# Grouped-query attention on one core: K by four heads, scores of two heads per matmul, by halves of the keys

## The chip, the core and the metric

The kernel runs on one core of a Trainium2 chip. TensorE (PE) multiplies; its weight loads have a queue of their own (PEld). VectorE (DVE), ScalarE (ACT) and GpSimd (POOL) do the rest, and SyncE (SP) issues every transfer between HBM and SBUF; 16 DMA engines carry them. The metric is the device time of one execution in microseconds, as the median of several runs. The kernel before takes 344.64 us (3 runs, 344.35 to 345.31).

## The reference

```python
B, Hq, Hkv, Sq, Sk, D = 16, 32, 8, 16, 2048, 128     # bfloat16
k = jnp.repeat(k, rep, axis=1)                        # rep = Hq // Hkv = 4
v = jnp.repeat(v, rep, axis=1)
scores = jnp.einsum("bhqd,bhkd->bhqk", q, k) * D ** -0.5
p = _softmax(scores, axis=-1)
return jnp.einsum("bhqk,bhkd->bhqd", p, v)
```

There are 16 x 8 = 128 K/V heads with 2048 keys each, 0.5 MB of K and 0.5 MB of V per head: 134 MB in all against 4 MB of Q and output. Each K/V head serves 4 query heads of 16 rows, so 64 query rows. Nothing is used twice, so all 134 MB go through SBUF once.

## The kernel before

Work goes by **pairs**: two K/V heads, 128 query rows, 64 pairs p in all. For a pair:

- SP loads K (`load_k`, L172; 1 MB, 8 KB in a row per partition) and V (`load_v`, L178; 1 MB, two rows of 4 KB per partition). The 64 partitions of one K head hold 32 keys each. V's last pair comes in two loads (`LASTV`). Q comes for eight pairs at once (`load_q`, 256 KB).
- DVE transposes K in blocks of 32 by 32 (`kt`, L315, two instructions of 1024 4-byte words per pair). A word is a pair of neighbouring bfloat16, so the two of a word, `e`, stay together, and `b` tells the two halves of 128 bytes apart. After it a 32-partition block of `KT` holds 32 words of D for its keys; the blocks 0 and 1 belong to the first head, 2 and 3 to the second, with different keys.
- GpSimd copies Q four times side by side into `Q4` (L165, once per eight pairs), so that PE's transposes (L246) put the same Q words in all four 32-partition blocks; ACT moves them to `QT` (L358).
- PE computes the scores S: for each of four accumulation steps (`b`, `e`) and two column halves `u`, four matmuls in tiles of 32 rows by 64 columns (L268 with a weight load, L224 on the loaded weights), one for each 32-partition block, into the whole of `S_ps` (4 of 8 PSUM banks).
- DVE scales by -1/sqrt(D), writes `Sneg` and accumulates the row minimum `nbias` (L333). ACT computes exp with that bias, writes `P` in bfloat16 and accumulates the row sum (L368). DVE inverts the sum (L324).
- PE transposes `P` in words (L280, eight per pair), ACT moves the result to `PT` (L378, two per pair). `PT` has `NPT` buffers, and PSUM has `NSTAGE` = 3 places for such transposes.
- PE multiplies `PT` with V (PV). In the wide form (L298) 16 matmuls of 256 columns compute each head's rows with both heads' V, and the useless halves are not read; ACT divides with two instructions (L391). In the narrow form (L304) 32 matmuls of 64 rows and 128 columns compute only what is needed; ACT divides with one (L395). The last `NFAST` = 12 pairs are narrow; the last pair is divided by DVE (L348).
- SP stores the 128 output rows (`store`, L198).

The order on PE and ACT is written out by a planner (L118 to L139) before the instructions are emitted. Iteration p puts S(p+1) first on PE, then PV(p-3) (`PVLAG`), then the transposes of P(p), and in four of eight iterations a part of the next Q. ACT gets exp(p), the division of p-3, the copies of P(p) and of Q. On DVE (L326 to L342) iteration p scales p, inverts p-1 and transposes K of p+2.

SP's order (L206 to L215) is fixed too: step t issues K of t, a Q if one is due, V of t-5 (`VLAG`), the store of t-12 (`SLAG`). SP waits in front of each until its buffer is free: K has 6 buffers (`NK`; free after both transposes), V has 8 (`NV`; free after PV), outputs 8. A wait there holds back all that is behind it. A load is one issue for all 16 DMA engines; its semaphore rises as each lands its share, so a load has landed when the last engine has.

Of the kernel before, what the change touches and what calls it, by code (L numbers as in the profile page):

```python
# [11 lines left out]
NK = 6  # L12
NV = 8
NKT = 2
NPT = 3
# [3 lines left out]
VLAG = 5  # L19
PVLAG = 3  # L20
SLAG = 12
QLEAD = 7
LASTV = ((0, 12), (12, 16))
NFAST = 12


def bass_standalone__gqa_softmax__sampling_kernel(
# [11 lines left out]
    NP = G // 2  # L39
    J = Sk // 128  # L40
# [9 lines left out]
    ident = sb("ident", [128, 128], BF16)  # L50
    ident4 = sb("ident4", [128, 128], F32)
    Kn = [sb(f"Kn{i}", [128, 2 * J * 128], BF16) for i in range(NK)]
# [5 lines left out]
    Sneg = [sb(f"Sneg{i}", [128, Sk], F32) for i in range(2)]  # L58
    P = [sb(f"P{i}", [128, Sk // 2], F32) for i in range(2)]
    PT = [sb(f"PT{i}", [128, J // 2, 128], F32) for i in range(NPT)]  # L60
    Osb = [sb(f"O{i}", [128, 128], BF16) for i in range(NO)]
    nbias = sb("nbias", [128, NP], F32)
# [15 lines left out]
    sem_max = sem("sem_max")  # L78
    sem_rec = sem("sem_rec")
# [10 lines left out]
    kf = k.rearrange("b h s d -> (b h s d)").rearrange("(n a x) -> n a x", n=NP, a=128)  # L90
    vf = v.rearrange("b h s d -> (b h) (s d)").rearrange("g (a x) -> a g x", a=128)

# [19 lines left out]
    def transposes(p):  # L112
        for h in range(2):
            u = stage("P", p, h)
            pe_prog.append(("PT", p, h, u))
            act_prog.append(("pe", p, h, u))
# [4 lines left out]
    for p in range(NP - 1):  # L121
        pe_prog.append(("S", p + 1))
        act_prog.append(("exp", p))
# [3 lines left out]
        transposes(p)  # L127
# [3 lines left out]
    for p in range(NP - 4, NP - 2):  # L131
        pv(p)
    act_prog.append(("exp", NP - 1))
    for p in range(NP - 4, NP - 2):
        norm(p)
    transposes(NP - 1)
# [15 lines left out]
    with nc.Block() as block:  # L152

        @block.gpsimd
        def _(gp):
            gp.iota(iota_t[:, :], [[1, 128]], base=0, channel_multiplier=-1).then_inc(sem_id, 1)
            gp.wait_ge(sem_id, 1)
            gp.tensor_scalar(ident[:, :], iota_t[:, :], 0.0, None, op0=ALU.is_equal).then_inc(sem_id, 1)
            gp.tensor_scalar(ident4[:, :], iota_t[:, :], 0.0, None, op0=ALU.is_equal).then_inc(sem_id, 1)
            for c in range(NQC):  # L160
                gp.wait_ge(sem_q[c % NQ], 16 * (c // NQ + 1))
                if c >= 1:
                    gp.wait_ge(sem_st, last_q[c - 1, 3] + 1)
                src = Qn[c % NQ][:, :, :].rearrange("p j (b x) -> p (j b) x", b=2)
                gp.tensor_copy(  # L165
                    Q4[:, :, :, :, :].rearrange("p j b r x -> p (j b) r x"),
                    src.unsqueeze(2).to_broadcast([128, 16, 4, 64]),
                ).then_inc(sem_q4, 1)

        @block.sync  # L170
        def _(sp):
            def load_k(p):  # L172
                s = p % NK
                if p >= NK:
                    sp.wait_ge(sem_kt, 2 * (p - NK) + 2)
                sp.dma_start(Kn[s][:, :], kf[p]).then_inc(sem_k[s], 16)
# [248 lines left out]
```

## Time and profile before

| | |
|---|---|
| median of 3 runs | 344.64 us (344.35 to 345.31) |
| the profiled execution | 344.92 us |
| its span in the profile | 343.1 us |
| instructions | 8217 |
| granted TensorE clock | 1.00 |
| mean rate of the loads | 405 GB/s |

The profile is of one execution. A row of the page names the line of the kernel, engine, operation, the tiles written and read, their partitions by elements and type, and the count; after the bar the total busy time and the mean duration in ns, then the time that the engine was idle just ahead of these instructions and what ended it. PE's matmuls are pipelined, so its busy time is an upper figure. A timeline line gives start, duration (merged, if it stands for several), engine, line and operation, and in brackets the idle time ahead of it with what ended it. The records of landings tell when each DMA engine had landed its share of a load. The chain that ended last, by engine:

```profile
PE 83%; DMA 5%; issue 4%; DVE 3%; ACT 1%; SPq 1%; POOL 1%; DVEq 0%; ACTq 0%
```

### The profile page before, as it was taken

The page shows a single profiled execution, that of the slowest core. Times are in us where ns is not written, and L with a number is a line of the kernel's source. Part 1 is how long each engine was busy: PE and PEld are TensorE (multiplying, and loading weights), DVE is VectorE, ACT ScalarE, POOL GpSimd, SP SyncE. Part 2 cuts the span into 40 slices and gives each one's busy share as a digit, 9 for nine tenths or more (in the row PEclk, how much of TensorE's full clock was granted, in tenths as well). Part 3 has the DMA queues.
Part 4 walks back from the last instruction along what each step waited for, and adds up shares of the span by engine and source line. Part 5 has one row for each costly group of instructions (what it writes and reads, how often), then busy time and mean ns, then how long its engine had stood idle before and what let it go on. Part 6 is the DMA issues. An engine that isn't in the chain of part 4 may idle for free.

```text
span 343.1 us, 8217 instructions
## 1 busy us (share of the span) xinstructions
PE 312.1 (91%) x3904; PEld 189.2 (55%) x2880; DVE 297.6 (87%) x321; ACT 291.8 (85%) x404; POOL 30.3 (9%) x15
## 2 busy tenths in 40 slices
PE   0757999999999999999999999999999999887784
PEld 0413656655665575557555755665565575454354
DVE  2289989999999999999899989998999898989840
ACT  1258899999999999999999999999988899877864
POOL 4500012000400004000300004000040000000000
PEclk9999999999999999999999999999999999999999
DMA  7999999999999999999999999999999999999993
GB/s 294 429 414 415 415 411 413 414 416 417 412 418 419 413 415 417 412 420 415 412 421 414 414 416 416 415 418 417 415 412 419 419 412 420 417 413 418 410 393 126
DMA packets 37300, 138.94 MB, mean 405 GB/s; under 512 B 11408, under 2 KB 11664, under 8 KB 29072
## 3 DMA queue, kind: packets, MB, share of 16 engines
q1 hardware_dynamic: 37264, 138.42, 99.6%
q8 instruction: 27, 0.44, 0.5%
q14 instruction: 9, 0.07, 0.1%
HBM read 136.31 MB, written 2.10 MB: 403 GB/s over the span
## 4 chain that ended last, share of the span: by engine, by line
PE 83%; DMA 5%; issue 4%; DVE 3%; ACT 1%; SPq 1%; POOL 1%; DVEq 0%; ACTq 0%
PE O_ps L298 28%; PE S_ps L268 18%; PE S_ps L224 15%; PE ST_ps L280 15%; PE ST_ps L246 5%; DMA Vb<-in_v_dram 4%; DVE KT L317 2%; PE O_ps L304 2%; DMA Qn<-in_q_dram 1%; DVE Sneg L333 1%; POOL Q L165 1%; SPq L204 1%; ACT P L368 1%; SPq L184 0%; PE S_ps L304 0%
## 5 line engine op out<-in xcount | busy, mean ns | idle before, releaser
L333 DVE TENSOR_SCALAR_CACHE_REDUCE Sneg<-S_ps 128x2048 f32<-128x2048 f32 x64 | 146.2, 2285 | 25.2 <-PE S_ps L224 24.0
L368 ACT ACTIVATE P<-Sneg,nbias 128x2048 bf16<-128x2048 f32 x64 | 158.8, 2481 | 7.7 <-DVE Sneg L333 6.1
L317 DVE STREAM_TRANSPOSE KT<-Kn 128x1024 f32<-128x1024 f32 x128 | 150.9, 1218 | 10.9 <-DMA Kn<-in_k_dram 10.9
L268 PE MATMUL S_ps<-KT,QT 32*64 32x512 bf16 x1024 | 103.4, 391 | 5.5 <-DVE Sneg L333 4.7
L224 PE MATMUL S_ps<-KT,QT 32*64 32x512 bf16 x1024 | 102.0, 385 | 0.0
L298 PEld LDWEIGHTS O_ps<-Vb,PT 128*128 128x128 bf16 x832 | 77.3, 98 | 44.0 <-issue 35.7
L298 PE MATMUL O_ps<-Vb,PT 128*128 128x256 bf16 x832 | 99.9, 273 | 1.5 <-issue 1.5
L378 ACT ACTIVATE PT<-ST_ps 128x512 f32<-128x512 f32 x128 | 69.5, 595 | 6.0 <-PE ST_ps L280 4.8
L280 PE MATMUL ST_ps<-ident,P 128*128 128x128 f32 x512 | 69.0, 278 | 2.8 <-ACT P L368 2.8
L268 PEld LDWEIGHTS S_ps<-KT,QT 32*64 32x64 bf16 x1024 | 30.0, 104 | 70.4 <-issue 61.6
L280 PEld LDWEIGHTS ST_ps<-ident,P 128*128 128x128 f32 x512 | 55.1, 141 | 12.1 <-ACT P L368 9.6
L391 ACT ACTIVATE O<-O_ps,rrec 64x128 bf16<-64x128 f32 x104 | 37.7, 363 | 15.8 <-PE O_ps L298 14.7
L165 POOL COPY Q<-Qn 128x4096 bf16<-128x4096 bf16 x8 | 28.8, 3602 | 224.2 <-PE ST_ps L246 143.9
L246 PE MATMUL ST_ps<-ident,Q 128*128 128x128 f32 x128 | 20.4, 291 | 10.1 <-POOL Q L165 10.1
L358 ACT ACTIVATE QT<-ST_ps 128x512 f32<-128x512 f32 x32 | 19.3, 603 | 10.0 <-PE ST_ps L246 10.0
L246 PEld LDWEIGHTS ST_ps<-ident,Q 128*128 128x128 f32 x128 | 16.4, 150 | 10.1 <-issue 10.1
L304 PE MATMUL O_ps<-Vb,PT 128*64 128x128 bf16 x288 | 9.8, 220 | 7.2 <-issue 7.2
L304 PEld LDWEIGHTS O_ps<-Vb,PT 128*64 128x64 bf16 x288 | 8.5, 110 | 12.9 <-issue 12.9
L324 DVE RECIPROCAL rrec<-rowsum 128x1 f32<-128x1 f32 x64 | 10.1, 158 | 3.1 <-ACT P L368 3.1
L368 ACT ACTIVATION_READ_ACCUMULATOR P<-Sneg,nbias 128x1 f32 x64 | 12.2, 190 | 0.0
L395 ACT ACTIVATE O<-O_ps,rrec 128x128 bf16<-128x128 f32 x9 | 3.3, 365 | 6.6 <-PE O_ps L304 6.6
L333 DVE DVE_READ_ACCUMULATOR Sneg<-S_ps 128x1 f32 x64 | 5.3, 83 | 0.0
(12 smaller groups left out, 10.2 us busy)
## 6 DMA issues: line engine op xcount, KB each, us to landing
Kn<-in_k_dram SPq DMA_DIRECT2D x64, 1024.0 KB, 15.9
Vb<-in_v_dram SPq DMA_DIRECT2D x63, 1024.0 KB, 17.7
Qn<-in_q_dram SPq DMA_DIRECT2D x8, 256.0 KB, 15.6
out_dram<-O SPq DMA_DIRECT2D x64, 32.0 KB, 15.9
Vb<-in_v_dram SPq DMA_DIRECT2D x1, 768.0 KB, 13.0
Vb<-in_v_dram SPq DMA_DIRECT2D x1, 256.0 KB, 12.5
```

The costliest lines, as they stand in the source:

```text
L165: gp.tensor_copy(Q4[:, :, :, :, :].rearrange("p j b r x -> p (j b) r x"), src.unsqueeze(2).to_broadcast([128, 16, 4, 64]),).then_inc(sem_q ...
L224: return pe.add_instruction(mybir.InstMatmult(name=nc.get_next_instruction_name(), engine=mybir.EngineType.PE, ins=[pe.lower_ap(rhs), pe.l ...
L246: ins = pe.transpose(dst[:, 128 * j:128 * (j + 1)], src[:, 4 * x + j, b, :], ident4[:, :])
L268: ins = pe.matmul(s_ap, w, x, start=(acc == 0), stop=(acc == 3))
L280: ins = pe.transpose(dst[:, 128 * t:128 * (t + 1)], P[p % 2][:, 128 * x:128 * (x + 1)], ident4[:, :])
L298: ins = pe.matmul(O_ps[:, 0:256], pt[:, j // 2, j % 2, :], Vb[p % NV][:, :, j, :], start=(j == 0), stop=(j == J - 1),)
L304: ins = pe.matmul(o_ap(p)[64 * g:64 * (g + 1), :], pt[:, j // 2, j % 2, 64 * g:64 * (g + 1)], Vb[p % NV][:, g, j, :], start=(j == 0), stop ...
L317: dve.transpose(KT[p % NKT][:, :].rearrange("p (t b e a x) -> p x e t b a", t=J // 2, b=2, e=2, x=2)[:, x, :, :, :, :], Kn[p % NK][:, :].b ...
L333: dve.tensor_scalar(Sneg[p % 2][:, :].rearrange("p (t h x) -> p h t x", t=8, h=2), S_ps[:, :].rearrange("p (h t x) -> p h t x", t=8, h=2), ...
L368: act.activation(P[p % 2][:, :].bitcast(BF16).rearrange("p (n y e) -> p n y e", n=16, e=2), Sneg[p % 2][:, :].rearrange("p (n e y) -> p n ...
L378: act.activation(PT[p % NPT][:, 4 * h:4 * (h + 1), :].rearrange("p t q -> p (t q)"), stage_ap(u), ACT.Copy,).then_inc(sem_ev, 1)
L391: ins = act.activation(Osb[p % NO][rows, :], O_ps[rows, 128 * g:128 * (g + 1)], ACT.Copy, scale=rrec[rows, p:p + 1])
```

## The change

K is loaded for **four heads** at a time: 2 MB, 16 KB in a row per partition, 32 loads in 3 buffers. A 32-partition block now belongs to one head and holds 64 keys per partition. So a block's words of D and keys are transposed as before, but the two blocks of 64 neighbouring partitions belong to two different heads, a pair. S is computed for two pairs (a **quad**, Q) by **halves of the keys**: step n = 2Q + x is half x of the keys of pairs 2Q and 2Q+1. One matmul takes 64 rows, the blocks of both heads of a pair, and 128 columns of weights. That the product of one head's queries with the other head's keys does not enter is seen to in Q's layout: each of `Q4`'s four copies is multiplied by a mask, 1 on the Q rows of its head and 0 on the others, so `QT` has zeros where query and key head differ. There are 64 steps S as before, each 16 matmuls of 512 columns (8 weight loads) in two tiles of 64 x 128, where there were 32 (16 weight loads) in four tiles of 32 x 64.

DVE now scales half a pair at a time (two instructions of 1024 per step instead of one of 2048), and after the second half takes the minimum of the two halves' minima for both pairs of the quad with one instruction, behind a wait for its own results. Only that releases exp of both pairs (`sem_nb`). The sums are inverted for two pairs at once. `Sneg` has 3 buffers instead of 2. exp reads its input in eight steps of 128 bytes, 32 times over, where it read two steps of 256 bytes, 64 times over; with that `P` has the keys in V's order.

The planner issues S two steps ahead instead of one, PV 4 behind instead of 3, V 6 behind instead of 5, stores 14 instead of 12; `PT` has 5 buffers instead of 3, V 7 instead of 8. Narrow are the last 8 pairs and before them each fourth. Q goes ahead of K in SP's first step. The last iterations are written out anew.

```diff
-NK = 6
-NV = 8
+NK = 3
+NV = 7
-NPT = 3
+NS = 3
+NPT = 5
-VLAG = 5
-PVLAG = 3
-SLAG = 12
+VLAG = 6
+PVLAG = 4
+SLAG = 14
-NFAST = 12
+NFAST = 8
+def both_heads(p, NP):
+    return p < NP - NFAST and p % 4 != 3
...
+    pe_prog.append(("S", 1))
+    for p in range(NP - 2):
+        pe_prog.append(("S", p + 2))
+        exp(p)
...
+    for p in range(NP - 2 - PVLAG, NP - 3):
         pv(p)
-    act_prog.append(("exp", NP - 1))
-    for p in range(NP - 4, NP - 2):
-        norm(p)
-    transposes(NP - 1)
+        if p < NP - 4:
+            norm(p)
+    exp(NP - 2)
+    exp(NP - 1)
+    ev = turn(NP - 2)
+    act_prog += ev
+    norm(NP - 4)
+    pv(NP - 3)
+    norm(NP - 3)
+    ev = turn(NP - 1)
+    act_prog += ev
     pv(NP - 2)
     norm(NP - 2)
     pv(NP - 1)
...
-                gp.tensor_copy(
-                    Q4[:, :, :, :, :].rearrange("p j b r x -> p (j b) r x"),
-                    src.unsqueeze(2).to_broadcast([128, 16, 4, 64]),
-                ).then_inc(sem_q4, 1)
+                for r in range(4):
+                    gp.tensor_scalar(
+                        Q4[:, :, :, r, :].rearrange("p j b x -> p (j b) x"), src,
+                        mask[:, r:r + 1], None, op0=ALU.mult,
+                    ).then_inc(sem_q4, 1)
...
+            def load_k(n):
+                s = n % NK
+                if n >= NK:
+                    sp.wait_ge(sem_kt, 4 * (n - NK) + 4)
+                sp.dma_start(Kn[s][:, :], kf[n]).then_inc(sem_k[s], 16)
...
+                            for y in range(2):
+                                rows = slice(64 * y, 64 * (y + 1))
+                                s_ap = S_ps[:, 512 * (2 * y + u):512 * (2 * y + u + 1)]
+                                w = qt[rows, b, e, 128 * (i + y):128 * (i + y + 1)]
+                                x = kt[rows, b, e, 2 * u:2 * (u + 1), :]
                                 if u == 0:
                                     ins = pe.matmul(s_ap, w, x, start=(acc == 0), stop=(acc == 3))
                                 else:
-                                    ins = matmul_on_loaded(s_ap, w, x, (32 * r, 64 * g), acc == 0, acc == 3)
+                                    ins = matmul_on_loaded(s_ap, w, x, (64 * y, 0), acc == 0, acc == 3)
...
+            for n in range(NP):
+                Q, x = divmod(n, 2)
+                dve.wait_ge(sem_s, n + 1)
+                for y in range(2):
+                    p = 2 * Q + y
+                    if x == 0 and p >= NS:
+                        dve.wait_ge(sem_exp, p - NS + 1)
+                    dve.tensor_scalar(
+                        Sneg[p % NS][:, 1024 * x:1024 * (x + 1)],
+                        S_ps[:, 1024 * y:1024 * (y + 1)], -scale, None,
+                        op0=ALU.mult, op1=ALU.min, accum_out=nhalf[:, x, p:p + 1],
+                    ).then_inc(sem_max, 1)
+                if x == 1:
+                    dve.wait_ge(sem_max, 2 * n + 2)
+                    pair = slice(2 * Q, 2 * Q + 2)
+                    dve.tensor_tensor(nbias[:, pair], nhalf[:, 0, pair], nhalf[:, 1, pair], op=ALU.min).then_inc(sem_nb, 1)
+                elif n >= 4:
+                    recip(Q - 2)
+                if n + 2 < NP:
+                    for e in range(2):
+                        kt(n + 2, e)
...
-                    act.wait_ge(sem_max, p + 1)
+                    act.wait_ge(sem_nb, p // 2 + 1)
...
-                        P[p % 2][:, :].bitcast(BF16).rearrange("p (n y e) -> p n y e", n=16, e=2),
-                        Sneg[p % 2][:, :].rearrange("p (n e y) -> p n y e", n=16, e=2), ACT.Exp,
+                        P[p % 2][:, :].bitcast(BF16).rearrange("p (n a m) -> p n a m", n=8, m=8),
+                        Sneg[p % NS][:, :].rearrange("p (n m a) -> p n a m", n=8, m=8), ACT.Exp,
```

The order of the instructions after the change, at the end, is on PE: S(63), PV(57), transposes of P(61), PV(58) to PV(60), transposes of 62, PV(61), transposes of 63, PV(62), PV(63); on ACT: exp(61), division 57, two copies of 61, divisions 58 and 59, exp(62), exp(63), two copies of 62, divisions 60 and 61, two copies of 63, division 62. In SP's order the last K load is followed by V of pairs 56 to 63.

## The prediction

> **What bounds the kernel now.** I read the page's busy shares first, then its DMA queues, then the busy time by stretches, then the timeline of the last 35 us.
>
> ```profile
> PE 312.1 (91%) x3904; PEld 189.2 (55%) x2880; DVE 297.6 (87%) x321; ACT 291.8 (85%) x404; POOL 30.3 (9%) x15
> q1 hardware_dynamic: 37264, 138.42, 99.6%
> q8 instruction: 27, 0.44, 0.5%
> L333 DVE TENSOR_SCALAR_CACHE_REDUCE Sneg<-S_ps 128x2048 f32<-128x2048 f32 x64 | 146.2, 2285 | 25.2 <-PE S_ps L224 24.0
> L368 ACT ACTIVATE P<-Sneg,nbias 128x2048 bf16<-128x2048 f32 x64 | 158.8, 2481 | 7.7 <-DVE Sneg L333 6.1
> L317 DVE STREAM_TRANSPOSE KT<-Kn 128x1024 f32<-128x1024 f32 x128 | 150.9, 1218 | 10.9 <-DMA Kn<-in_k_dram 10.9
> L165 POOL COPY Q<-Qn 128x4096 bf16<-128x4096 bf16 x8 | 28.8, 3602 | 224.2 <-PE ST_ps L246 143.9
> ```
>
> Four engines are at 85% or more and the loads are at 99.6%, so shares alone don't name the bound. The stretches do (time, then busy time of PE, PEld, DVE, ACT, POOL, then clock, DMA share, GB/s):
>
> ```profile
> 95.90:135.40 39.50, 39.50 (x465) 24.05 (x337) 37.17 (x41) 37.04 (x53) 3.60 (x1) 1.00 1.02 415
> 254.10:293.90 39.80, 38.59 (x452) 24.18 (x332) 36.18 (x40) 35.74 (x52) 1.06 (x1) 1.00 1.02 415
> 293.90:343.00 49.10, 36.91 (x696) 22.88 (x572) 34.01 (x39) 35.63 (x47) 0.00 (x0) 1.00 0.91 362
> ```
>
> Up to about 235 us PE is never idle: eight iterations take 39.5 us, 4.94 each. The loads run at 415 GB/s throughout. A pair is 2.10 MB of K and V plus 0.07 MB of Q and output, so loading it takes 5.2 us: PE is the faster of the two. It starts late, catches up, and from about 290 us DVE waits for K at each pair. So **the loads set the end**; PE sets it only in so far as it must have caught up. The end itself:
>
> ```profile
> 323.14 2.37 DVE L317 STREAM_TRANSPOSE KT<-Kn 128x1024 f32<-128x1024 f32 x2 [0.47 <-DMA Kn<-in_k_dram]
> 330.95 2.29 DVE L333 TENSOR_SCALAR_CACHE_REDUCE Sneg<-S_ps 128x2048 f32<-128x2048 f32 x1 [3.17 <-PE S_ps L224]
> 333.85 2.46 ACT L368 ACTIVATE P<-Sneg,nbias 128x2048 bf16<-128x2048 f32 x1
> 339.30 1.09 PE L304 MATMUL S_ps<-Vb,PT 128*64 128x128 bf16 x32 [0.73 <-DMA Vb<-in_v_dram]
> 340.53 0.35 DVE L348 TENSOR_SCALAR O<-S_ps,rrec 128x128 bf16<-128x128 f32 x1 [3.92 <-PE S_ps L304]
> ```
>
> The last K is taken at 323.1, the last scores are scaled at 331, the last exp ends at 336.3, and PE still waits 0.73 us for the last V. That V has landed whole at 339.85 (landing records of the trace). The rest, 3.3 us, is PV, division and store. The profiled execution took 344.92 us around a span of 343.1 (1.8 us outside it) and is 0.28 above the median, 344.64. I sum against the span.
>
> **The loads: -2.8 us.** In the first 30 us, with a full queue and no stores, a K megabyte lands 2.49 us after its predecessor and a V megabyte 2.55. Each of 16 engines has 8 packets of 8 KB in the former, 16 of 4 KB in the latter: 0.06 us for 8 packets, 7.5 ns a packet. K in 16 KB rows drops 4 packets per engine and megabyte, 64 times: 1.9 us. Bounds: nothing, if rows are cut at 8 KB, and 2.3 us by the packets' own times (309 ns for 8 KB, 159 for 4 KB: 9 ns a packet). Secondly, the 16 engines land the first load within 0.45 us of each other (5.18 to 5.63) but the last within 6.5 (333.31 to 339.85); the lag grows in steps, with the 27 instruction loads. S goes from 32 matmuls and 16 weight loads to 16 and 8 (-1536 instructions), ten more pairs take the narrow PV with 32 and 32 instead of 16 and 16 (+320), and the doubled scaling and the four Q products add some 120. That is 7120 of 8217, 13% less, hence 0.9 of the 6.5 us (bounds 0 and 6.5).
>
> The 2.49 us between landings are little more than a megabyte's eight packets, 8 x 309 ns, so in a queue that is never empty a load by itself costs nothing that shows. The Trainium skill (SBUF — State Buffer, The DMA setup-cost knee) says that every transfer pays about 2 us whatever its size; by that rule 32 loads fewer would be worth up to 64 us, and this trace does not agree.
>
> **The start: +0.6 us.** K's buffers are released by four heads. SP issues in order: the fourth K load stands behind the four transposes of the first, the fifth behind those of the second, and V behind both. Ahead of the fifth are 2 Q, 4 K of 2 MB and 2 V. At the rates above, from a first landing of data at 3.1 us, they have landed at 29.2 (a Q load is 0.67, 8 packets of 84 ns). The fifth is issued when the transposes of key half 3 are done. Those follow S(0) and S(1), which follow Q4. GpSimd first makes the mask with eight small operations (0.23 to 0.55 us for those like them: until 4.2 us; Q itself, now ahead of K, lands at 3.8). Four products of 1024 elements replace a copy of 4096. Unseen; at the copy's rate they are 3.6 us in all, at that of the 128-element compare (528 ns) 16.9. I take the copy's 0.88 ns an element plus the compare's remaining 0.42 us, 1.3 each, 5.2 in all, nearest to the copy, which has like size and type: Q4 ends at 9.4 (9.94 now), S(0) starts at 13.9 (14.5 now). The cold S(0) takes to 17.6, scaling to 20.1, transposes of half 2 to 22.4 (S(1) beside them), scaling with the minimum to 25.05, transposes of half 3 to 27.3. From issue to the first data took 2.4 us at the start, so the queue runs dry for 27.4 + 2.4 - 29.2 = 0.6 us. Behind that it keeps two rounds of 10 us of work. Each us by which Q4 is later adds one us to this gap, and the gap goes straight to the end.
>
> The Trainium skill (GPSIMD Engine Reference, Elementwise — side-by-side cycle accounting) speaks against this part: it states about 2.6 cycles an element for two inputs, and 1.03 for short bodies that the port bounds. An estimate by the former (1.2 GHz, 2.2 us a product) puts the sum some 4 us higher, by the latter it stays; no operation like it is in this trace.
>
> **The iterations: no change in the end, if they stay at 4.94 us.** PE: S keeps eight waves of 512 columns (four tiles of 32x64 now, 0.225 us a wave; two of 64x128 afterwards). No row shows such a pair: bounds are 0.225 and, one after the other, 0.45 a wave, +1.8 us per pair; I take 0.225, since the rows show that tiles in different rows do overlap. A narrow PV takes 1.09 instead of 1.85 us; one in four gives -0.19 a pair. DVE: two halves of 1024 for one 2048 (2285 ns; 1024-element transposes 1218) add about 0.13 a pair, and the minimum of the halves (reciprocal: 158 ns) with its wait 0.2 every second time. Behind that wait stand two transposes. DVE's loop was 4.53 where PE had little to do (22.7 to 36.3 us) and becomes 4.8. ACT loses 0.09 a pair. But exp is released for two pairs at once, so ACT's second exp comes late and PE's transposes wait for it in iterations with Q work. I take 4.94 as before, bounds 4.8 and 5.15. Key half 8 is transposed from 48.9 us on; 54 iterations later half 62 comes up at 315.3.
>
> **The end: +3.7 us.** After the last K load now come 6 V loads, landing over 16.7 us; afterwards 8, so 2 x 2.6 more: 21.95. The last V lands at 339.85 - 2.8 + 0.6 = 337.65, so the last K, T, at 315.7, which the iterations meet. From T, with the rows above: transposes 2.4; scaling of half 61, queued behind them, to 4.8, minimum 5.0; transposes of 63 to 7.3; meanwhile S(62) 4.9 to 6.9; scaling 62 to 9.7; S(63) to 11.75; PV(57), transposes 61, PV(58) to 15.0; division 58 (0.37), PV(59), division 59 to 17.05; only then, in ACT's order, exp 62 and exp 63 to 22.1, though the minimum was there at 14.5; two copies of 62, divisions 60 and 61, two copies of 63 to 25.1; PV(63) to 26.2; and from there 2.75 as now (340.39 to 343.14). The end is T + 28.95 = 344.65: the last V is 7.0 us old by then instead of 3.3. What was hidden under V's landing, the last score chain, no longer is.
>
> **Sum.** Loads -2.8, start +0.6, end +3.7: +1.5 us on 343.14, so 346.4 for the profiled execution and 346.1 against the median.
>
> **Rivals.**
> 1. *GpSimd or the iterations hold it.* For: products with a pointer operand are unseen, and the pair release of exp leaves 0.3 us of room. Against: 32 us of idle time around GpSimd's later copies, and the copy is fast. At 2.6 us a product, the middle of the bounds from the two rows, S(0) comes 5.2 us later: 351.3. Iterations of 5.05 bring half 62 to 321.6: 352. It decides from a Q4 above 6 us or iterations above 4.95.
> 2. *No slower: the lagging DMA engine.* If fewer instruction loads leave the slowest engine no later than the fastest, T is up to 5.6 us earlier, 310.1, and the end 339.0, where the iterations allow it (4.8: half 62 at 308.1): 340.5. Midway, 342.3 to 343. It decides from T at 313.2, which also needs iterations below 4.89. For: the lag is the largest unexplained size. Against: PE, whose instructions shrink, still loads most.
> 3. *About the same: exp is cheaper.* Its read order is now eight steps of 128 bytes. A copy of 512 takes 595 ns and one of 128 365, so 2048 would be 1.51 at that slope; the row has 2.48. Two exps lie on the end's chain: up to -1.9, 344.2. Dearer by the same: 348.
> 4. *It doesn't do what it says.* Packets stay at 8 KB: +1.9, 348.0. Tile pairs run in turn: 64 x 1.8 us, about 460.
>
> **How the numbers follow.** Forecast, with 4's first half: 0.40. Rival 1: 0.15. Tile pairs in turn: 0.03. These are slower: 0.58. Rival 3, same: 0.20. Rival 2, faster: 0.22. A measurement of this kernel tells about 0.3% from no change, 343.6 to 345.7. The range goes from the middle of rival 2's span, 341.5, to rival 1's first price, 351.5; GpSimd's far end and the turns are left out. The forecast's own range is 345.7 to 348.
>
> **What would show it.** K packets of 16 KB at about 610 ns; some 23 instruction loads; S(0) near 13.9; a gap below 1 us in the slices around 28 us; PE 39.5 us per eight iterations; the last K wait of DVE near 316, the last V landed some 7 us before the end, and exp 62 starting on a division's release. If PE waits for V at the end, the tail is mis-sized; if DVE never waits for K late, the iterations are the bound.

## The result and the profile after

The changed kernel takes **423.83 us** (4 runs, 422.55 to 425.34), the kernel before on the same chip 344.63. The ratio is 1.230, with a 95% interval of 1.225 to 1.234. The forecast was 346.1 with a range up to 351.5. Of the 79 us the prediction has 1.5. That the direction came out right says little: it rested on 1.5 us, and most of the loss comes from a price that the sum did not have.

The profiled execution took 422.55 us, its span is 420.5. First the page: busy time by engine, the two queues that the prediction spoke of, the chain that ended last, and the groups that answer to those shown of before.

```profile
PE 318.2 (76%) x3040; PEld 182.8 (43%) x2528; DVE 305.6 (73%) x449; ACT 371.6 (88%) x394; POOL 92.6 (22%) x44
...
q1 hardware_dynamic: 32656, 138.42, 85.8%
q8 instruction: 22, 0.36, 0.3%
...
ACT 61%; issue 19%; PE 15%; POOL 3%; DVE 1%; DMA 1%; ACTq 0%; DVEq 0%; POOLq 0%
...
L411 ACT ACTIVATE P<-Sneg,nbias 128x2048 bf16<-128x2048 f32 x64 | 249.3, 3895 | 10.9 <-DVE nbias L380 9.9
L372 DVE TENSOR_SCALAR_CACHE_REDUCE Sneg<-S_ps 128x1024 f32<-128x1024 f32 x128 | 153.4, 1218 | 88.0 <-PE S_ps L257 52.3
L352 DVE STREAM_TRANSPOSE KT<-Kn 128x1024 f32<-128x1024 f32 x128 | 150.8, 1217 | 8.8 <-DMA Kn<-in_k_dram 8.8
L198 POOL TENSOR_SCALAR Q<-Qn,mask 128x1024 bf16<-128x1024 bf16 x32 | 90.4, 2842 | 226.7 <-PE ST_ps L279 226.4
```

The loads no longer set the end: their share falls from 99.6% to 85.8%. PE and DVE have about as much to do as before (6 and 8 us more) and a share smaller by 14 or 15 points. ACT has 80 us more to do. GpSimd has 62 more, but is in the chain with 3%, the length of its first products. The chain that ended last, PE's by 83% before, is now ACT's by 61%. One row explains it: **exp costs 3895 ns instead of 2481**, 64 times 1.41 us, 90.5 us of ACT's time. Scaling and transposes of K cost what the prediction took.

The middle of the run (start and end of the stretch, its length, busy time of PE, PEld, DVE, ACT, POOL, then clock, DMA share, GB/s), and who waits for whom (us in total, times, longest), for DVE, PE and SP's queue:

```profile
100.00:200.00 100.00, 81.87 (x756) 47.17 (x621) 77.49 (x114) 95.53 (x104) 22.60 (x8) 0.98 0.93 354
```

```profile
DVE Sneg L372 <- ACT P L411: 35.7, 29, 1.5
...
DVE KT L352 <- DMA Kn<-in_k_dram: 8.8, 1, 8.8
...
PE ST_ps L313 <- ACT P L411: 65.5, 55, 2.6
...
SPq L209 <- DVE KT L352: 247.7, 29, 16.5
```

ACT is busy 95.5 of 100 us. PE's transposes wait for exp 55 times, DVE's scaling waits 29 times for a place in `Sneg` that exp still reads, and SP holds K back for buffers that DVE frees late. DVE waits for K only once, at the very start. The starts of the exps in the trace are 6.12 us apart on average (pairs 10 to 42); before it was 4.94.

The second thing to see is at the start and the end:

```profile
3.59 11.31 POOL L198 TENSOR_SCALAR Q<-Qn,mask 128x1024 bf16<-128x1024 bf16 x4 [0.36 <-DMA Qn<-in_q_dram]
8.80 4.62 DVE L352 STREAM_TRANSPOSE KT<-Kn 128x1024 f32<-128x1024 f32 x4 [8.80 <-DMA Kn<-in_k_dram]
...
19.32 0.40 PE L301 MATMUL S_ps<-KT,QT 64*128 64x512 bf16 x2 [0.78 <-ACT QT L402]
...
406.49 0.37 ACT L438 ACTIVATE O<-O_ps,rrec 128x128 bf16<-128x128 f32 x1 [1.27 <-PE O_ps L337]
...
406.75 3.77 ACT L411 ACTIVATE P<-Sneg,nbias 128x2048 bf16<-128x2048 f32 x1
...
410.53 3.83 ACT L411 ACTIVATE P<-Sneg,nbias 128x2048 bf16<-128x2048 f32 x1
```

GpSimd's four products take 11.3 us, not 5.2; S(0) starts at 19.3, not 13.9. At the end exp 62 does start on the release of division 59, as forecast, and the two exps then take 7.6 us.

### The profile page after: what moved, and what is told of

It reads as the page before. It is cut to its first block, busy times and chain, and to the rows that moved or that the text cites. A ratio compares the mean times of both kernels' runs of the same rounds, so it can differ in the third digit from the quotient of the medians.

```text
span 420.5 us, 7083 instructions
## 1 busy us (share of the span) xinstructions
PE 318.2 (76%) x3040; PEld 182.8 (43%) x2528; DVE 305.6 (73%) x449; ACT 371.6 (88%) x394; POOL 92.6 (22%) x44
## 3 DMA queue, kind: packets, MB, share of 16 engines
q1 hardware_dynamic: 32656, 138.42, 85.8%
## 4 chain that ended last, share of the span: by engine, by line
ACT 61%; issue 19%; PE 15%; POOL 3%; DVE 1%; DMA 1%; ACTq 0%; DVEq 0%; POOLq 0%
ACT P L411 50%; ACT PT L421 10%; PE ST_ps L313 10%; POOL Q L198 3%; PE ST_ps L279 1%; DVE Sneg L372 1%; PE S_ps L301 1%; PE S_ps L257 1%; ACT QT L402 1%; DMA Qn<-in_q_dram 1%; PE O_ps L337 1%; PE O_ps L331 0%; PE S_ps L337 0%; ACT O L434 0%; ACT O L438 0%
## 5 line engine op out<-in xcount | busy, mean ns | idle before, releaser
L411 ACT ACTIVATE P<-Sneg,nbias 128x2048 bf16<-128x2048 f32 x64 | 249.3, 3895 | 10.9 <-DVE nbias L380 9.9
L372 DVE TENSOR_SCALAR_CACHE_REDUCE Sneg<-S_ps 128x1024 f32<-128x1024 f32 x128 | 153.4, 1218 | 88.0 <-PE S_ps L257 52.3
L198 POOL TENSOR_SCALAR Q<-Qn,mask 128x1024 bf16<-128x1024 bf16 x32 | 90.4, 2842 | 226.7 <-PE ST_ps L279 226.4
L301 PE MATMUL S_ps<-KT,QT 64*128 64x512 bf16 x512 | 104.4, 398 | 17.0 <-DVE Sneg L372 10.1
L257 PE MATMUL S_ps<-KT,QT 64*128 64x512 bf16 x512 | 103.5, 394 | 0.0
L421 ACT ACTIVATE PT<-ST_ps 128x512 f32<-128x512 f32 x128 | 69.6, 595 | 15.8 <-PE ST_ps L313 11.3
L331 PE MATMUL O_ps<-Vb,PT 128*128 128x256 bf16 x672 | 80.7, 273 | 0.0
L331 PEld LDWEIGHTS O_ps<-Vb,PT 128*128 128x128 bf16 x672 | 62.4, 98 | 35.1 <-issue 28.5
L301 PEld LDWEIGHTS S_ps<-KT,QT 64*128 64x128 bf16 x512 | 27.3, 95 | 87.3 <-issue 71.2
L402 ACT ACTIVATE QT<-ST_ps 128x512 f32<-128x512 f32 x32 | 19.3, 604 | 15.1 <-PE ST_ps L279 14.9
L434 ACT ACTIVATE O<-O_ps,rrec 64x128 bf16<-64x128 f32 x84 | 30.0, 357 | 1.3 <-PE O_ps L331 0.8
L279 PEld LDWEIGHTS ST_ps<-ident,Q 128*128 128x128 f32 x128 | 16.9, 156 | 15.0 <-issue 15.0
L337 PEld LDWEIGHTS O_ps<-Vb,PT 128*64 128x64 bf16 x608 | 17.6, 110 | 12.2 <-issue 12.2
L337 PE MATMUL O_ps<-Vb,PT 128*64 128x128 bf16 x608 | 20.6, 221 | 1.1 <-ACT O L438 1.1
L360 DVE RECIPROCAL rrec<-rowsum 128x2 f32<-128x2 f32 x32 | 5.1, 160 | 11.5 <-ACT P L411 11.5
```

What stands on the lines that cost most here:

```text
L198: gp.tensor_scalar(Q4[:, :, :, r, :].rearrange("p j b x -> p (j b) x"), src, mask[:, r:r + 1], None, op0=ALU.mult,).then_inc(sem_q4, 1)
L257: return pe.add_instruction(mybir.InstMatmult(name=nc.get_next_instruction_name(), engine=mybir.EngineType.PE, ins=[pe.lower_ap(rhs), pe.l ...
L279: ins = pe.transpose(dst[:, 128 * j:128 * (j + 1)], src[:, 4 * x + j, b, :], ident4[:, :])
L301: ins = pe.matmul(s_ap, w, x, start=(acc == 0), stop=(acc == 3))
L331: ins = pe.matmul(O_ps[:, 0:256], pt[:, j // 2, j % 2, :], Vb[p % NV][:, :, j, :], start=(j == 0), stop=(j == J - 1),)
L337: ins = pe.matmul(o_ap(p)[64 * g:64 * (g + 1), :], pt[:, j // 2, j % 2, 64 * g:64 * (g + 1)], Vb[p % NV][:, g, j, :], start=(j == 0), stop ...
```

## The experiments

The theory after the result: **(A)** exp's new read order makes one exp 1.41 us dearer, ACT had no room for that in any iteration, and so ACT became the bound. The rival **(B)**: exp is dear in the changed kernel for something beside the order, such as its three buffers or the work around it. Under either, part of the loss may be the start.

### The order of exp, in both kernels and alone

Three kernels change only the order in which exp goes through its data. The changed kernel with the order of before:

```diff
-P[p % 2][:, :].bitcast(BF16).rearrange("p (n a m) -> p n a m", n=8, m=8),
-Sneg[p % NS][:, :].rearrange("p (n m a) -> p n a m", n=8, m=8), ACT.Exp,
+P[p % 2][:, :].bitcast(BF16).rearrange("p (n y e) -> p n y e", n=16, e=2),
+Sneg[p % NS][:, :].rearrange("p (n e y) -> p n y e", n=16, e=2), ACT.Exp,
```

> The changed kernel with one edit: exp reads its input and writes P in the order of the kernel before (two steps of 256 bytes, 64 times over, instead of eight of 128 bytes). The keys of P are then not in V's order, so what comes out is not the attention; all sizes, counts and waits stay. Theory A (the read order alone makes exp dear, and exp makes ScalarE the bound of every iteration): exp falls from 3895 to about 2480 ns, ScalarE from 371.6 us busy to about 281, the loads take the bound back. By the prediction's sum, with the 5.5 us by which GpSimd's products are later than forecast, the time is 351.6 (348 to 354). Rival B (exp is dear for another reason in the changed kernel, such as where its buffers lie or what runs beside it): exp stays near 3.9 us and the time near 424.

The changed kernel with exp straight through (`P[p % 2][:, :].bitcast(BF16)` from `Sneg[p % NS][:, :]`):

> The changed kernel with exp reading and writing straight through; the keys of P are not in V's order, so what comes out is not the attention. Theory A: exp costs less still, 280 ns and 2048 times the 0.83 ns of ScalarE's copies, 2.0 us; but the loads, not ScalarE, are then the bound, so beyond the two exps in the chain of the end nothing more is won over the same kernel with the old order: 350.6 (347 to 353). Rival B: exp stays near 3.9 us and the time near 424. Rival C (the iterations are bound by ScalarE even with exps of 2.48 us): this one is faster than the one with the old order by up to 64 times 0.48, 31 us.

The kernel before with the order of the changed one, the first diff the other way round:

> The kernel before with one edit: exp reads and writes in the order of the changed kernel (eight steps of 128 bytes); the keys of P are then not in V's order, so what comes out is not the attention. Theory A: exp rises from 2481 to about 3895 ns, eight iterations of ScalarE from 37.0 to 48.3 us, so an iteration takes 6.05 us instead of 4.94 and 64 of them with start and end about 412 (405 to 420). Rival B (the order is not what makes exp dear): exp stays at 2.48 us and the time at 344.6.

| kernel | exp, ns | iteration, us | time, us |
|---|---|---|---|
| before | 2481 | 4.94 | 344.63; 344.97 beside the three edited ones |
| before, new order | 3889 | 6.09 | 413.26 |
| changed | 3895 | 6.12 | 423.83 |
| changed, order of before | 2482 | 5.065 | 357.63 |
| changed, in order | 2003 | 4.978 | 352.49 |

(The iteration is the mean distance of exps 10 to 42 in the trace.) The order alone carries exp's price from one kernel to the other, and with it the bound; B has fallen. The kernel before becomes the same picture with one edit (chain and exp), and the changed kernel has the old price back with one (exp):

```profile
ACT 61%; issue 21%; PE 14%; DMA 1%; POOL 1%; DVE 1%; SPq 0%; DVEq 0%; ACTq 0%
...
L368 ACT ACTIVATE P<-Sneg,nbias 128x2048 bf16<-128x2048 f32 x64 | 248.9, 3889 | 7.5 <-DVE Sneg L333 6.1
```

```profile
L411 ACT ACTIVATE P<-Sneg,nbias 128x2048 bf16<-128x2048 f32 x64 | 158.8, 2482 | 11.3 <-DVE nbias L380 10.3
```

The first two expectations were 6 and 2 us too low. With the order of before, the loads did not take the bound back: DVE again waits for K only once. The iterations hold it, at 5.065 us and not at the 4.94 that I had kept; rival C of the second run was right in kind (5.1 us faster, by iterations), far below its upper end.

### What an exp costs by its order

> No attention: single instructions on constant data, one after another, each behind the end of the last, and zeros stored. Exps of 128x2048 by read order; the words between steps and their number are varied. Theory A1 (each element read from another place than its neighbour costs the same, however far and however many): plain 2.0 us, two steps 2.48 only at 256 bytes, all forms of eight steps 3.9. Theory A2 (the distance counts: steps within the same 16 or 64 bytes are free): eight steps of 8 or 16 bytes near 2.0, eight of 64, 128 and 256 bytes 3.9, thirty-two of 128 the same 3.9. Theory A3 (the number of places counts, because two can be held but eight can't): two steps 2.48 at any distance, four between, eight and thirty-two 3.9 and more. Reading in order and writing in steps of 16 bytes: 2.0 if only the read side costs, 3.9 if the write side does. Reads from PSUM: in steps as dear as from SBUF, or 2.0. GpSimd's product of 1024 elements: 2.8 us with a mask operand as in the changed kernel; with a number 2.8 if the arithmetic costs, 1.3 or less if the operand does; a copy of 1024 near 1.0. VectorE's product and ScalarE's scaled copy of the same 1024: below 1.3. VectorE's transposes with a written step of 8 words: 1.2 us as with neighbouring words, or more.

Exps of 2048 elements, one after another, on constant data. In the order of the lines: straight through, two places 256 bytes apart, four of 128 bytes, eight of 128, eight of 16, eight of 8, thirty-two of 128; then from PSUM, eight of 128 bytes; then read straight and written in steps of 16 bytes.

```profile
85.82 2.00 ACT L130 ACTIVATE P_plain<-X,bias 128x2048 bf16<-128x2048 f32 x1
...
94.33 2.45 ACT L130 ACTIVATE P_twostepsof<-X,bias 128x2048 bf16<-128x2048 f32 x1
...
125.26 3.79 ACT L130 ACTIVATE P_foursteps<-X,bias 128x2048 bf16<-128x2048 f32 x1
...
140.90 3.73 ACT L130 ACTIVATE P_eightsteps<-X,bias 128x2048 bf16<-128x2048 f32 x1
...
187.14 3.92 ACT L130 ACTIVATE P_eightsteps<-X,bias 128x2048 bf16<-128x2048 f32 x1
...
203.30 2.21 ACT L130 ACTIVATE P_eightsteps<-X,bias 128x2048 bf16<-128x2048 f32 x1
...
212.64 3.74 ACT L130 ACTIVATE P_thirtytwosteps<-X,bias 128x2048 bf16<-128x2048 f32 x1
...
236.44 1.97 ACT L130 ACTIVATE P_psumeightsteps<-XP,bias 128x2048 bf16<-128x2048 f32 x1
...
244.81 9.35 ACT L130 ACTIVATE P_writeeightsteps<-X,bias 128x2048 bf16<-128x2048 f32 x1
```

It is the number of places that counts, as in A3, with A2 at short distance. Two places cost 2.45 us at 256, 128 and 16 bytes alike; four, eight and thirty-two about 3.75. So four are already as dear as eight, where A3 had them between, and the reason that A3 gives is not shown. The next element in the same 16 bytes is nearly free (2.21). From PSUM eight steps of 128 bytes cost nothing. Writing in steps is the dearest by far. In both attention kernels the exp in eight steps takes 3.89 us, 0.16 more than alone; where those 0.16 come from was not tried.

The Trainium skill (SBUF — State Buffer, Specifications (TRN2)) gives SBUF 16-byte lines, says that full bandwidth needs at least two hits per line, and that each crossing to a new line is penalised. The 8-byte and 16-byte forms agree (2.21 with two hits, 3.92 with one). The page gives the penalty no size, and it has not one size here: with two alternating places every element crosses to another line too, but the exp costs 2.45 and not 3.73.

Other groups of the same run, with both exps that read PSUM:

```profile
L102 POOL COPY G_copyfour<-Qn 128x4096 bf16<-128x4096 bf16 x4 | 14.4, 3601 | 8.3 <-DVE XP L61 8.1
L104 POOL TENSOR_SCALAR G_pointer<-Qn,msk 128x1024 bf16<-128x1024 bf16 x4 | 11.4, 2844 | 0.4
L106 POOL TENSOR_SCALAR G_number<-Qn 128x1024 bf16<-128x1024 bf16 x4 | 11.1, 2769 | 0.3
L74 DVE STREAM_TRANSPOSE Z_trby<-KT 128x1024 f32<-128x1024 f32 x4 | 8.1, 2014 | 0.1
...
L78 DVE TENSOR_SCALAR_CACHE_REDUCE D_writeby<-XP 128x1024 f32<-128x1024 f32 x4 | 7.9, 1986 | 0.1
L130 ACT ACTIVATE P_psumplain<-XP,bias 128x2048 bf16<-128x2048 f32 x4 | 7.9, 1968 | 0.1
L130 ACT ACTIVATE P_psumeightsteps<-XP,bias 128x2048 bf16<-128x2048 f32 x4 | 7.9, 1967 | 0.1
L72 DVE STREAM_TRANSPOSE Z_tr<-KT 128x1024 f32<-128x1024 f32 x4 | 5.0, 1246 | 42.5 <-POOL G_narrowcopy L108 42.4
L76 DVE TENSOR_SCALAR_CACHE_REDUCE D_plain<-XP 128x1024 f32<-128x1024 f32 x4 | 4.9, 1224 | 0.1
L82 DVE TENSOR_SCALAR_CACHE_REDUCE D_readby<-XP 128x1024 f32<-128x1024 f32 x4 | 4.9, 1224 | 0.1
...
L108 POOL COPY G_narrowcopy<-Qn 128x1024 bf16<-128x1024 bf16 x4 | 4.2, 1041 | 0.2
...
L86 DVE TENSOR_SCALAR G_dve<-Qn,msk 128x1024 bf16<-128x1024 bf16 x4 | 1.9, 486 | 0.1
```

GpSimd's product costs its arithmetic, not the mask operand: 2.77 us with a number, 2.84 with the operand, 1.04 for a copy of the same size. VectorE does the same product in 0.49. And VectorE's scaling may read PSUM in eight steps at no cost (1224 ns, as straight through), while written steps cost it 1986.

### The order moved to VectorE, then the start

So the order can go into the scaling, which reads PSUM anyway, and exp runs straight through with P in V's order.

```diff
-Sneg[p % NS][:, 1024 * x:1024 * (x + 1)],
-S_ps[:, 1024 * y:1024 * (y + 1)], -scale, None,
+Sneg[p % NS][:, 1024 * x:1024 * (x + 1)].rearrange("p (t a m) -> p t a m", t=4, m=8),
+S_ps[:, 1024 * y:1024 * (y + 1)].rearrange("p (t m a) -> p t a m", t=4, m=8), -scale, None,
...
-P[p % 2][:, :].bitcast(BF16).rearrange("p (n a m) -> p n a m", n=8, m=8),
-Sneg[p % NS][:, :].rearrange("p (n m a) -> p n a m", n=8, m=8), ACT.Exp,
+P[p % 2][:, :].bitcast(BF16),
+Sneg[p % NS][:, :], ACT.Exp,
```

> The changed kernel with the keys put in order by VectorE's scaling, which reads PSUM in eight steps of 128 bytes and writes straight on; exp then reads and writes straight through. All work is done as in the changed kernel. Theory A (steps cost ScalarE only where it reads SBUF; VectorE reads PSUM in steps at no cost, 1224 ns both ways by itself): exp 2.0 us, scaling 1.21 us, time that of the run with exp in order, 352.5 (351 to 354). Rival B (beside the matmuls that write the other banks, the stepped reads are dearer, up to the 1.99 us of the stepped writes): an iteration of VectorE rises by up to 1.5 us and the time to as much as 440.

Measured: 350.74 us, ratio to before 1.017 (1.014 to 1.020). Scaling and exp in its profile:

```profile
L372 DVE TENSOR_SCALAR_CACHE_REDUCE Sneg<-S_ps 128x1024 f32<-128x1024 f32 x128 | 150.7, 1213 | 24.5 <-PE S_ps L257 24.3
...
L411 ACT ACTIVATE P<-Sneg,nbias 128x2048 bf16<-128x2048 f32 x64 | 128.2, 2004 | 11.8 <-DVE nbias L380 10.8
```

The order is free there. The whole 73 us between this and the changed kernel is the place of one permutation. Next, on top of it, GpSimd leaves out the first Q, and VectorE makes its four products ahead of the first transposes of K:

```diff
-for c in range(NQC):
+for c in range(1, NQC):
...
+dve.wait_ge(sem_id, 8)
+dve.wait_ge(sem_q[0], 16)
+for r in range(4):
+    dve.tensor_scalar(
+        Q4[:, :, :, r, :].rearrange("p j b x -> p (j b) x"),
+        Qn[0][:, :, :].rearrange("p j (b x) -> p (j b) x", b=2),
+        mask[:, r:r + 1], None, op0=ALU.mult,
+    ).then_inc(sem_q4, 1)
```

> The kernel with the order on VectorE, and with the first Q's four products on VectorE (0.49 us each by itself) instead of GpSimd (2.84 us each). Theory A (the late Q4 is the rest of the loss against the kernel before): Q4 ends near 6.3 instead of 14.9 us, S(0) starts near 11.5 instead of 19.3, where K's first transposes end; the gap in the loads near 30 us goes, and the 8 us go straight to the end, where the iterations are the bound: 344.5; where the loads become the bound, the last K lands near 315 and the end is 29 us later less 1 us for two shorter exps: 343.1 and 1.8 outside the span, 344.9. Together 343 to 347. Rival B (iterations of 4.98 us are held by something that the start does not move, such as places in PSUM): the iterations keep their distance to the loads, and of the 8 us less than 3 are won, 349.5 or more.

The same edit alone, in the changed kernel, with exp still dear:

> The changed kernel, exp as dear as it is there, with only the first Q's products on VectorE. Theory A (ScalarE is the bound from the first exp on, so start and exp add up): the first exp comes 5.3 us earlier, the same as in the pair of kernels with cheap exps, and the time is 418.5 (417.5 to 419.5). Rival B (the start is hidden where exp is the bound): 423.8.

Measured: 344.42 and 419.38, or 0.998 and 1.215 of before. The start is worth 6.4 us beside a cheap exp and 5.0 beside the dear one (by the ratios; their intervals overlap), so the two causes add up. With a cheap exp the products now take 1.67 us, S(0) starts at 11.35, the gap in the loads is gone. The first exp is 5.3 us earlier, not 8: most of the first S run at little more than half speed, 0.61 to 0.66 us for a pair of matmuls instead of 0.40. After that the gain stays to the end, 5.0 us at exp 62: iterations of 4.978 us hold it, with DVE waiting for K only at the start (first two lines of the timeline, then the stretches with the clock in the third column from the right, then DVE's wait: us, times, longest).

```profile
3.52 1.67 DVE L365 TENSOR_SCALAR Q<-Qn,mask 128x1024 bf16<-128x1024 bf16 x4 [3.52 <-DMA Qn<-in_q_dram]
...
11.35 0.61 PE L301 MATMUL S_ps<-KT,QT 64*128 64x512 bf16 x2 [2.37 <-DVE KT L352]
```

```profile
10.00:15.00 5.00, 3.54 (x16) 0.53 (x8) 3.62 (x5) 0.00 (x0) 5.00 (x2) 1.00 1.01 433
15.00:20.00 5.00, 2.55 (x16) 0.58 (x8) 4.59 (x6) 0.00 (x0) 5.00 (x3) 0.81 1.01 433
20.00:25.00 5.00, 2.44 (x14) 0.47 (x6) 4.43 (x7) 1.86 (x1) 1.02 (x1) 0.50 0.96 404
```

```profile
DVE KT L352 <- DMA Kn<-in_k_dram: 3.7, 1, 3.7
```

The clock falls to 0.81 and 0.50 while S is slow, but does not account for it: S(0), from 11.35 to 14.9 us, is as slow where the clock shows 1.00, and in a later trace with the same start (the one with the last exps between the divisions, below) nearly all pairs of the first three S take 0.61 to 0.66 us while the clock shows 1.00 from 10 to 30 us. The gain differs by execution, too: in the six traces with this start the first exp comes at 21.7 to 23.9 us, in the four that have the changed kernel's start at 28.4 to 29.0.

The order on VectorE was tried in the kernel before too, where exp read from two places 256 bytes apart:

```diff
-Sneg[p % 2][:, :].rearrange("p (t h x) -> p h t x", t=8, h=2),
-S_ps[:, :].rearrange("p (h t x) -> p h t x", t=8, h=2), -scale, None,
+Sneg[p % 2][:, :].rearrange("p (t h y e) -> p h t y e", t=8, h=2, e=2),
+S_ps[:, :].rearrange("p (h t e y) -> p h t y e", t=8, h=2, e=2), -scale, None,
...
-P[p % 2][:, :].bitcast(BF16).rearrange("p (n y e) -> p n y e", n=16, e=2),
-Sneg[p % 2][:, :].rearrange("p (n e y) -> p n y e", n=16, e=2), ACT.Exp,
+P[p % 2][:, :].bitcast(BF16),
+Sneg[p % 2][:, :], ACT.Exp,
```

> The kernel before with one thing changed: VectorE's scaling reads PSUM with neighbouring keys 256 bytes apart and writes P's order, so that exp reads straight through. Theory A: exp 2.0 instead of 2.48 us; the scaling as before (2.29 us); ScalarE loses 31 us of busy time, but the loads set the end, so only the one exp in the chain of the end counts: 0.5 us less, 344.4 against 344.9 on this chip. Rival B (ScalarE's share of the iterations matters all along): several us less. Rival C (stepped reads of single words cost VectorE): scaling above 2.4 us and the time above 346.

Measured: 344.93, ratio 0.9995 (0.9985 to 1.0005). exp falls to 2003 ns, scaling stays at 2281, ACT loses 31 us of busy time, and nothing comes of it, since the loads set the end there. A first fear, that the stepped reads cost VectorE, is out; half a microsecond from the one exp at the end does not show either.

### The end and the iterations

The three last terms of the prediction can be tested now that exp is no longer in the way. First the last exps, queued behind divisions 58 and 59. On ACT: exp 62, division 58, exp 63, division 59:

```diff
-    for p in range(NP - 2 - PVLAG, NP - 3):
-        pv(p)
-        if p < NP - 4:
-            norm(p)
+    pv(NP - 6)
     exp(NP - 2)
+    norm(NP - 6)
+    pv(NP - 5)
     exp(NP - 1)
+    norm(NP - 5)
...
```

> The kernel with order and first Q on VectorE, and the last iterations in another order: exp 62 ahead of division 58, exp 63 ahead of division 59, the transposes of 62 ahead of PV(60), and PV(60) in a bank of its own. Theory A (the last two exps are late because they queue behind divisions, as the prediction's end has it): they start 2 to 2.5 us earlier against the last K's landing, and the end comes 2 us earlier: about 342.5 (341 to 344). Rival B (the last V or the iterations hold the end): no gain, within 0.5 us of the kernel without it.

Measured: 345.38, no gain (0.9989 to 1.0023 of before; without the new order 0.9973 to 0.9994). exp 62 did start 4.8 us behind exp 61 instead of 7.1. But PE waited 2.1 us for division 58, now behind an exp, and came back slow (first the timeline, then the stretch with the clock in the third column from the right):

```profile
332.77 1.74 PE L336 MATMUL O_ps<-Vb,PT 128*64 128x128 bf16 x32 [2.08 <-ACT O L445]
...
334.43 1.97 PE L312 MATMUL ST_ps<-ident,P 128*128 128x128 f32 x8
```

```profile
330.00:335.00 5.00, 2.92 (x61) 2.62 (x56) 0.45 (x5) 4.91 (x7) 0.00 (x0) 0.80 0.83 311
```

Both instructions take 1.09 us at full clock; in these 5 us it is 0.80. Without the wait, in the order division 58, exp 62, division 59, exp 63, again with PV(60) in a bank of its own (against the kernel with order and first Q on VectorE, as the diff above):

```diff
-    for p in range(NP - 2 - PVLAG, NP - 3):
-        pv(p)
-        if p < NP - 4:
-            norm(p)
+    pv(NP - 6)
+    norm(NP - 6)
+    pv(NP - 5)
     exp(NP - 2)
+    norm(NP - 5)
     exp(NP - 1)
+    pv(NP - 4)
...
```

> The kernel with order and first Q on VectorE, and the last iterations in a third order: division 58 first, then exp 62, division 59, exp 63, with PV(60) in a bank of its own. Theory A (in the order with exp 62 ahead of division 58 the 2.8 us won by the exps went to PE: it waited 2.1 us for that division and then ran at a lower granted clock): exp 62 starts 1.8 us earlier than in the kernel without a new order, at 331.3, PE waits under 1 us at a time, transposes of 62 and 63 take 1.1 us each, and the end is 1.5 us earlier: 342.9 (342 to 343.8). Rival B (something behind the exps holds the end, the last V or the divisions): within 0.5 us of 344.4.

Measured: 343.12, ratio 0.994 (0.992 to 0.995). exp 62 starts 5.5 us behind exp 61, 1.6 earlier than without a new order, and PE's transposes take 1.09.

Then the iterations. The narrow PV goes to those pairs whose PV shares an iteration with Q's transposes:

```diff
-    return p < NP - NFAST and p % 4 != 3
+    return p < NP - NFAST and p % 8 in (2, 3, 4, 5)
```

> As the kernel with the last exps between the divisions, and the narrow PV moved and doubled: of eight pairs the four whose PV comes in an iteration with a part of Q. Theory A (an iteration takes 4.98 us on average because those with Q's transposes are PE's, about 5.2 to 5.3, and the others VectorE's, about 4.7): the narrow form takes 0.84 us off the former, the average falls to about 4.75, and the loads become the bound: DVE waits for K again, the last K lands near 315.5 and the end is 26 to 27 us behind: 341.5 to 343.5 with 1.8 outside the span, 342.3. Rival B (the narrow form's 450 instructions more cost what they save, in instruction loads and stalls of PE's queue): 4.9 us or more an iteration, 343 to 346.

Measured: **342.63**, ratio 0.993 (0.992 to 0.994), the lowest median of all versions. Against the version without it that is 0.5 us less, and the intervals of the two overlap, so a gain in time is not shown. What the trace shows is that the bound changed. Iterations fall to 4.747 us up to pair 26, then the loads take over at 5.15 to 5.28 (the queue on the page, and DVE's waits):

```profile
q1 hardware_dynamic: 32656, 138.42, 99.5%
```

```profile
DVE KT L352 <- DMA Kn<-in_k_dram: 16.2, 16, 3.7
```

DVE waits for K 16 times, as in the kernel before (12 times). With the loads as the bound, the packets can be weighed: each K load cut in two with 8 KB a row.

```diff
-sp.dma_start(Kn[s][:, :], kf[n]).then_inc(sem_k[s], 16)
+for x in range(2):
+    half = slice(4096 * x, 4096 * (x + 1))
+    sp.dma_start(Kn[s][:, half], kf[n][:, half]).then_inc(sem_k[s], 16)
```

> The kernel with the narrow PV beside Q, with each K load cut in two of 1 MB and 8 KB a row. Theory A (the packets' gain is real: 2 MB of K land in 4.90 us with 16 KB rows and in 2 x 2.49 with 8 KB): K lands 0.08 us later per 2 MB, 2.6 us over 32, and where the loads are the bound the time rises by 2 to 2.6 us: about 344.7. Rival B (the iterations are the bound all the same): the time stays within 0.7 us.

Measured: 345.07, so 2.44 us more. In the trace 2 MB of K land 4.89 us apart with 16 KB packets and 2 x 2.485 with 8 KB; the last V lands at 336.8 and at 338.6. The gain is real, and it is what brings this version below the kernel before (345.26 beside it): with 8 KB packets nothing would be left. The edit doubles the number of K loads along with the packets, so the two are not told apart by the time; by the packets' own times (611 ns for 16 KB, 309 for 8 KB) eight of the former are 0.06 us shorter than sixteen of the latter, most of the 0.08 us per 2 MB.

## Why the prediction was wrong, step by step

**The step that failed is rival 3, exp's read order.** It was priced at "Two exps lie on the end's chain: up to -1.9, 344.2. Dearer by the same: 348". In the sum itself it has no price at all: the iterations' "ACT loses 0.09 a pair" leaves exp at its old 2.48 us without a reason. Two errors are in the sentence on the rival.

- *The path.* A dearer exp was counted twice, at the end, and not 64 times. The prediction's own table of stretches shows what forbids that: in eight iterations of 39.5 us ACT is busy 37.04, so it has 0.31 us of room a pair. Any exp dearer by more than that makes ACT the bound of all iterations. It even wrote that the pair release "leaves 0.3 us of room", and did not carry exp's price there.
- *The size.* The slope of the copies served as a bound on one side and was mirrored to make the other, +0.97 us. Nothing in the trace supports the mirror: the one row with a stepped read, exp itself, was dearer than the slope, which spoke for more. It was +1.41. The slope was off for exps in order too: 2.00 us measured, not 1.51. With the mirrored 3.45 us on every iteration the sum would have been 37.04 / 8 + 0.97 = 5.60 us, 42 us over 64, about 388; with the measured price 6.04 an iteration, and 6.12 was measured.

The other terms:

- **Loads, -2.8.** Packets -1.9 with bounds 0 and 2.3: the pair of kernels with 16 and 8 KB gives 2.44, a little over the upper bound. Instruction loads fell from 27 to 22 and instructions to 7083 (7120 forecast). Their 0.9 us was not tested alone. In three later versions with the order on VectorE the last V lands over 5.3, 5.0 and 4.9 us instead of 6.5, with 22, 22 and 24 instruction loads: about what was forecast, but not in proportion to their number (in the changed kernel itself, whose queue runs dry again and again, it lands within 0.6). In the trace of before, four of the 27 loads, at 33.5, 128.9, 229.7 and 324.5 us, bring most of it: around them the spread goes from 0.44 to 1.99, 2.05 to 3.49, 3.72 to 4.89 and 5.38 to 6.52 us. Rival 2, which had this lag gone, did not come.
- **Start, +0.6.** One product costs 2.84 us instead of 1.3, inside the bounds (3.6 to 16.9 for four) and above the middle that rival 1 took. The fourth product decides: Q4 at 14.9, S(0) at 19.3, the fifth K issued at 31.3, and as that K has landed from 38.45 on, 4.9 us after its data begin, the queue is dry for 4.3 us behind the landing of the second V (29.2). S(0) took 2.0 us and not the 3.7 of the forecast's cold one, so that the gap grew by less than Q4's delay of 5.5. By itself the start is worth 5.0 to 6.4 us. The chain of steps was right and this term mis-sized.
- **Iterations, 4.94.** With exp as before 5.065 (bounds 4.8 to 5.15): PE's transposes wait for exp 18 times, 13.4 us, as the text feared. Over 62 iterations that is 7.8 us, and this kernel has the iterations as its bound, not the loads. With the start that is about 13 us, where 11.5 lie between the 346.1 and the 357.6 of the changed kernel with the order of before. Rival 1 named both conditions, and its two prices (+5.2 and +5.9) together would give 357.2: beside the read order, this is the rival that came.
- **End, +3.7.** exps 62 and 63 behind division 59: as forecast, and the order between the divisions, with a bank for PV(60), wins 1.6 us of it (by the ratios).
- **Rival 4.** K's packets are 16 KB (4096 at a median of 611 ns), and the two tiles of 64 x 128 do overlap: S is 16 matmuls of some 0.4 us, in pairs 0.23 us apart, so 1.8 in all.

What each part is worth: the median, its ratio to the kernel before beside it, and the step between the ratios times 345 us. The step of 0.3 is within the noise.

| kernel | us | ratio | step, us |
|---|---|---|---|
| changed | 423.83 | 1.230 | |
| exp in the order of before | 357.63 | 1.037 | -66.6 |
| exp in order, the keys ordered by VectorE | 350.74 | 1.017 | -6.8 |
| and the first Q's products on VectorE | 344.42 | 0.998 | -6.4 |
| and the last exps between the divisions | 343.12 | 0.994 | -1.6 |
| and the narrow PV beside Q | 342.63 | 0.993 | -0.3 |
| and K in packets of 8 KB | 345.07 | 1.000 | +2.4 |

Of the idea of the change, the larger loads gain 2.4 us of 345; what the wider tiles for S gain was not measured by itself. The order of the keys and the mask on GpSimd, which the change needs, were put on the wrong engines. What stays open is why PE runs its first S slower when they start earlier, which in the profiled pair keeps 2.7 of the 8 us won there; this was not tried.

## What to carry to other kernels

Where an engine is busy 37.0 of 39.5 us, price every change of its instructions per iteration first, the read order among them, and only then at the end. An access order that the trace does not show has no symmetrical bound around a neighbour's price: measure it by itself, and put a permutation where its steps are free, here into VectorE's read of PSUM. A cheaper instruction is worth nothing where its engine is not the bound: the same edit gave 7 us in one kernel and none in the other.

## What the runs showed of the hardware

- ScalarE from SBUF, 2048 words: 2.00 us in order, 2.45 with two alternating places 16, 128 or 256 bytes apart, 3.72 to 3.92 with four and more 16 bytes or more apart, 2.21 if two neighbours share 16 bytes. From PSUM 1.97, in order and in eight steps of 128 bytes.
- Writing 2-byte results in steps of 16 bytes: 9.35 us for the same exp, nearly five times the price. VectorE writing words in steps of 32 bytes: 1.99 instead of 1.22 us, and its transposes 2.01 instead of 1.25.
- GpSimd: 1024 bfloat16 multiplied by a number 2.77 us, copied 1.04. The Trainium skill (GPSIMD Engine Reference, Elementwise — side-by-side cycle accounting) has 1.03 cycles an element for short bodies and 2.6 for two inputs. The prediction's estimate by the latter was 2.2 us; a product with one input and a number is dearer than that, 2.77.
- PE after waits of over 2 us: with the last exps first, eight transposes follow a wait of 2.1 us in 1.97 us instead of 1.09, at a granted clock of 0.80 in that stretch. The slow matmuls need not come at once: with the dear exp and the first Q on VectorE, a wait of 2.6 us is followed by eight transposes in 1.09 us, and the next eight, 3.8 us later, take 1.97. Why is not shown.
